# An attention-and-experts kernel: both column tiles of the weights-times-values products read all 128 key rows

## The chip, the cores and the metric

The kernel runs on one core of a Trainium2 chip. The metric is the device time of one execution in microseconds (us); lower is better.

## What is computed

Two parts follow one another. The first is a gated linear attention (an mLSTM): for 4 batches, 8 heads, 768 time steps and 40 features it runs the recurrence below. The second is a soft mixture of 8 experts with 4 slots each over the 3072 rows that the first part gives.

```python
for t in range(S):
    m_new = np.maximum(f_gate[:, :, t] + m, i_gate[:, :, t])
    f_stab, i_stab = np.exp(f_gate[:, :, t] + m - m_new), np.exp(i_gate[:, :, t] - m_new)
    C = f_stab * C + i_stab * outer(vt, kt)
    n = f_stab * n + i_stab * kt
    y[:, :, t] = sigmoid(o_gate[:, :, t]) * (C @ qt) / np.maximum(np.abs(n @ qt), 1.0)
...
logits = x @ phi
d = softmax(logits, over rows);  slot_input = d.T @ x
slot_out[e] = np.maximum(slot_input[e] @ w1[e], 0.0) @ w2[e]
out = softmax(logits, over slots) @ slot_out
```

## The kernel before

The recurrence is worked in chunks of 128 time steps. A step `i` of the main loop is one chunk of one batch: `c = i // 4` is the chunk, `i % 4` the batch, 24 steps in all (`NSTEP`). All 8 heads of a step go together as 4 pairs (`HP`), `j` is the pair and `e` the head in it. Within a chunk a query attends to the keys of its own chunk, up to its own time, by a matrix of weights; to everything earlier it attends through a state of 40 x 41 numbers a head (the last column carries the normaliser).

What one step does:

- `expo(i)` (L294): two products on TensorE (L302) build the logarithms of the decay weights in the PSUM tile `pe`, keys on the partitions, queries on the columns, in two halves of 64 queries. For the first 64 queries only keys 0 to 63 are worked out; rows 64 to 127 of that half of `pe` were set to -1e30 once, at the start (L173). ScalarE then takes the exponential of all 128 rows of both halves into `ew[i]` (L304), so that the rows of later keys hold zeros. From step 4 on, a further product (L312 and L313 in chunks 0 to 2, L316 after) and exponential (L317) give the decay of the state for each query. In chunks 0 to 2 the factors of these products, `LLt` and `RR`, are written by ScalarE (L267) and VectorE (L270) in the step before; later ones come by DMA.
- `scores(i)` (L331): keys times queries, 16 matmuls into `psc`. `mix(i)` (L345, VectorE) multiplies them into `ew[i]`.
- `mix_q(i)` (L340, GpSimd) multiplies the queries by the state's decay.
- `pv(i)` (L383): the products that the change touches. For each pair `j` it adds up, in a PSUM tile `ph` with the 128 queries on the partitions, the part from the state (L393, 104 rows, 82 columns, from step 4 on) and the part from the chunk's own keys (L398, one head at a time, 41 columns: 40 features of the values and the normaliser). The 128 queries are cut in two column tiles of 64 (`u`, `NT = 2`, `TW = 64`), which use the left and the right half of TensorE's columns (`tile_position=(0, 64 * u)`) and write the lower and the upper half of the partitions of `ph`. For `u = 0`, the first 64 queries, L398 reads only keys 0 to 63 (`k = LH = 64` rows); for `u = 1` it reads all 128.
- `post1`, `post2` (L403, L419, VectorE) and `gate` (L430, GpSimd) divide and gate the result; `xtr` (L438) transposes it (L444) and ScalarE copies it out (L447).
- `keys(i)` (L350, GpSimd) and `state(i)` (L362) give the state's increment: for each pair two products with 128 rows and 41 columns (L367 with 64 columns of weights into partitions 0 to 63 of `pst`, L369 with 40 into partitions 64 to 103). `state_ops` (L371) adds it to the state.
- Every fourth step the experts' part takes up four finished steps: `moe_logits` (L452), `moe_psl` (L505), transposes (L496, L522, L543).

The order of all instructions is written out by hand. The loop (L666) issues, in step `i`: loads, `expo(i+2)`, `mix(i+1)`, `gate(i-1)`, `mix_q(i+1)`, `keys(i+1)`, `state_ops(i-1)`, the experts' parts, `pv(i)`, `scores(i+2)`, `state(i)`, `xtr(i-1)`, then `post1(i)` and `post2(i)`. The last two steps stand after the loop (L745 on), with `pv` into the PSUM tiles `phe` and `bk`. After them come the experts' two layers (`up` L874, `down` L900) and the output (`combine` L922). Loads are issued on the SP queue.

Each float32 product appears in the trace as two passes, each with a weight load (LDWEIGHTS, engine PEld) and a MATMUL (engine PE). A pair `j` of `pv` from step 4 on thus has 4 passes of L393 and 8 of L398.

Of the kernel before, what the change touches and what calls it, by code (L numbers as in the profile page):

```python
# [16 lines left out]
LH = L // 2  # L17
NT = 2
TW = L // NT
# [3 lines left out]
V1 = D + 1  # L23
# [44 lines left out]
def kernel(ctx: ExitStack, tc: tile.TileContext, qk, kv, og, g0, g1, g2, consts, cb, w1, w2, out):  # L68
    nc = tc.nc
    P = 128  # L70
# [287 lines left out]
    def v_of(i, h):  # L358
        return KV[i % NK][:, DM + h * V1:DM + (h + 1) * V1]
# [23 lines left out]
    def pv(i, ph_=None):  # L383
        w = ew[i]
        if ph_ is None:
            ph_ = pp.tile([P, 512], F32, tag="ph", name=f"ph{i}")

        for j in range(HP):
            c0 = 2 * j * V1
            if i >= B:  # L390
                for u in range(NT):
                    z = slice(TW * u, TW * u + TW)
                    nc.tensor.matmul(ph_[z, c0:c0 + 2 * V1], w[0:104, 2, j, z], St[0:104, i % B, j], start=True, stop=False,  # L393
                                     tile_position=(0, TW * u))
            for e in range(2):
                for u in range(NT):
                    z, k = slice(TW * u, TW * u + TW), LH if TW * u < LH else P
                    nc.tensor.matmul(ph_[z, c0 + e * V1:c0 + (e + 1) * V1], w[0:k, e, j, z], v_of(i, 2 * j + e)[0:k],  # L398
                                     start=i < B, stop=i < B or e == 1, tile_position=(0, TW * u))
        phs[i] = ph_[:, 0:H * V1].rearrange("p (h d) -> p h d", h=H)  # L400
        nqs[i] = ph_[:, 512 - H:512]
# [208 lines left out]
    emit(nxt)  # L610
    state(0)
    pv(0, pp.tile([P, 512], F32, tag="pm", name="ph0", bufs=2))
    load_kv(3)
    emit(state_ops(0))
# [51 lines left out]
    for i in range(1, NL - 1):  # L666
# [40 lines left out]
        if i > GRP and i % GRP == 2:  # L707
            moe_acc(gi, psl)
        pv(i)
        scores(i + 2)  # L710
        state(i)
# [26 lines left out]
    i = NL - 1  # L738
# [13 lines left out]
    nc.gpsimd.memset(xy[:, DM:DM + 1], 1.0)  # L752
    nc.gpsimd.memset(xr[:, :, DM:DM + 1], 1.0)
    pv(i)
    scores(NL + 1)
    pl4 = moe_pl(gl - 1, "pm")
# [33 lines left out]
    j = NL + 1  # L790
# [279 lines left out]
```

## Time and profile before

| | |
|---|---|
| median of 3 runs | 370.34 us (365.2 to 373.87) |
| the profiled execution | 364.1 us |
| span of its instructions | 362.3 us |
| mean granted TensorE clock | 0.592 of 2.4 GHz |
| PE busy | 340.0 us (94%) |
| PEld busy | 239.8 us (66%) |
| VectorE, ScalarE, GpSimd busy | 108.7, 97.1, 77.2 us |

The span is what the profile shows; 1.8 us of the execution lie around it. PE is TensorE's matmuls and PEld its weight loads, which overlap them. Matmuls are pipelined, and the profile models their ends, so that a busy PE is not a PE at its peak: starts of successive matmuls say more than their durations. The granted clock has two levels here, 0.5 (1.2 GHz) and 1.0 (2.4 GHz).

### The profile page before, as it was taken

What the parts mean: (1) busy time and instruction counts of PE and PEld (TensorE: products, weight loads), DVE (VectorE), ACT (ScalarE), POOL (GpSimd) and SP (SyncE); (2) the same over time, 40 slices, a digit from 0 to 9 for tenths busy, and PEclk for the clock granted to TensorE, in tenths of its full rate; (3) what the DMA queues carried; (4) which work ended last, traced back from release to release, by engine and by line L of the source; (5) the groups of instructions that cost most, each with busy time, mean ns of one, the idle gap of its engine ahead of it and who ended that gap; (6) DMA issues with size and microseconds to landing.
All of it is one profiled execution on the core that took longest, in us unless ns stands there. A gap on an engine that the chain in (4) does not pass through costs nothing.

```text
span 362.3 us, 6383 instructions
## 1 busy us (share of the span) xinstructions
PE 340.0 (94%) x2609; PEld 239.8 (66%) x2609; DVE 108.7 (30%) x311; ACT 97.1 (27%) x234; POOL 77.2 (21%) x95
## 2 busy tenths in 40 slices
PE   5999988987989899999999999999999999999991
PEld 2777866756567677567677577677686677552681
DVE  7534304201423331213231214133141212233251
ACT  6734053031321303411221402232212200121041
POOL 4602334200213320203320204220233210011000
PEclk9556555555555558555555556578865555558996
DMA  8653435042134603414631613842504525390067
GB/s 246 195 167 111 145 125 175 30 133 71 60 85 139 203 18 121 136 47 144 192 100 50 207 29 108 276 134 80 190 17 145 183 62 193 118 352 3 2 214 224
DMA packets 27308, 47.36 MB, mean 131 GB/s; under 512 B 3168, under 2 KB 18400, under 8 KB 27280
## 3 DMA queue, kind: packets, MB, share of 16 engines
q1 hardware_dynamic: 27280, 46.96, 40.5%
q8 instruction: 21, 0.34, 0.4%
q14 instruction: 7, 0.06, 0.1%
HBM read 42.72 MB, written 4.23 MB: 130 GB/s over the span
## 4 chain that ended last, share of the span: by engine, by line
PE 75%; DVE 1%; ACT 1%; issue 1%; DVEq 0%
PE ph L398 25%; PE psc L338 9%; PE ph L393 7%; PE pe L302 4%; PE pt L444 4%; PE pst L367 3%; PE pso L905 3%; PE phh L877 2%; PE pl L452 2%; PE phe L398 2%; PE bk L398 2%; PE psl L505 2%; PE pq L316 1%; PE po L935 1%; PE bk L877 1%; PE pst L369 1%
## 5 line engine op out<-in xcount | busy, mean ns | idle before, releaser
L398 PE MATMUL ph<-KVt,ew 64*64 64x41 f32 x704 | 125.1, 302 | 0.0
L398 PEld LDWEIGHTS ph<-KVt,ew 64*64 64x64 f32 x704 | 94.4, 190 | 33.2 <-issue 11.8
L434 POOL TENSOR_TENSOR Xt<-sig,den 128x320 f32<-128x320 f32 x20 | 15.1, 756 | 176.2 <-DVE sig L423 98.4
L447 ACT COPY xT<-pt 128x384 f32<-128x384 f32 x23 | 11.0, 479 | 154.8 <-PE pt L444 154.8
L338 PE MATMUL psc<-KQt 64*128 64x128 f32 (+1 forms) x384 | 49.4, 434 | 0.4 <-DVE ew L348 0.4
L393 PE MATMUL ph<-St,ew 104*64 104x82 f32 x288 | 46.0, 342 | 1.0 <-DVE sig L423 1.0
L338 PEld LDWEIGHTS psc<-KQt 64*128 64x128 f32 (+1 forms) x384 | 42.3, 321 | 3.7 <-DVE ew L348 1.1
L393 PEld LDWEIGHTS ph<-St,ew 104*64 104x64 f32 x288 | 29.6, 197 | 10.4 <-issue 9.8
L348 DVE TENSOR_TENSOR ew<-psc,ew 128x1024 f32<-128x1024 f32 x24 | 29.3, 1223 | 21.4 <-PE psc L338 19.6
L407 DVE TENSOR_REDUCE ph<-ph 128x8 f32<-128x8 f32 x22 | 3.8, 172 | 98.2 <-PE ph L398 98.2
L304 ACT ACTIVATE ew<-pe 128x512 f32<-128x512 f32 x48 | 26.0, 593 | 23.5 <-PE pe L302 22.2
L343 POOL TENSOR_TENSOR ew<-KQt,ew 104x512 f32<-104x512 f32 x20 | 25.4, 1271 | 11.0 <-ACT ew L317 9.7
L302 PE MATMUL pe<-RRt,LLt 128*64 128x512 f32 (+1 forms) x24 | 12.9, 637 | 10.7 <-ACT LLt L267 7.9
L367 PEld LDWEIGHTS pst<-KVt,KRt 128*64 128x64 f32 x160 | 18.5, 221 | 4.5 <-issue 3.4
L367 PE MATMUL pst<-KVt,KRt 128*64 128x41 f32 x160 | 21.5, 310 | 0.0
L444 PE MATMUL pt<-cst,Xt 128*128 128x128 f32 x63 | 18.3, 433 | 0.0
L353 POOL TENSOR_TENSOR KRt<-KVt,rl 128x320 f32<-128x320 f32 x20 | 15.7, 787 | 9.6 <-ACT rl L325 9.4
L369 PE MATMUL pst<-KVt,KRt 128*40 128x41 f32 x160 | 16.1, 276 | 0.0
L302 PEld LDWEIGHTS pe<-RRt,LLt 128*64 128x64 f32 (+1 forms) x24 | 5.1, 234 | 15.1 <-ACT LLt L267 8.2
L378 DVE SCALAR_TENSOR_TENSOR St<-St,rl,pst 104x82 f32<-104x82 f32 x64 | 14.7, 292 | 0.0
L369 PEld LDWEIGHTS pst<-KVt,KRt 128*40 128x40 f32 x160 | 13.1, 170 | 0.0
L526 DVE TENSOR_REDUCE rmx<-pd 128x4 f32<-128x128 f32 x4 | 1.2, 292 | 39.6 <-PE pd L522 39.6
(230 smaller groups left out, 348.3 us busy)
## 6 DMA issues: line engine op xcount, KB each, us to landing
w<-in_w_dram SPq DMA_DIRECT2D x20, 512.0 KB, 5.0
KVt<-in_kv_dram SPq DMA_DIRECT2D x24, 324.0 KB, 3.1
KQt<-in_qk_dram SPq DMA_DIRECT2D x24, 320.0 KB, 3.8
w<-in_w_dram SPq DMA_DIRECT2D x10, 640.0 KB, 6.5
sig<-in_og_dram SPq DMA_DIRECT2D x6, 640.0 KB, 6.3
out_dram<-ob SPq DMA_DIRECT2D x5, 384.0 KB, 2.8
KQt<-in_w_dram SPq DMA_DIRECT2D x2, 640.0 KB, 6.0
out_dram<-ob SPq DMA_DIRECT2D x2, 512.0 KB
```

The costliest lines, as they stand in the source:

```text
L302: nc.tensor.matmul(pe[0:x, n], l[0:k, n * LH:n * LH + x], r[0:k, :, n * LH:n * LH + LH], start=True, stop=True)
L304: nc.scalar.activation(w[:, 0:2, :, n * LH:n * LH + LH].rearrange("p e j t -> p j e t"), pe[:, n].rearrange("p (j e) t -> p j e t", e=2), ...
L338: nc.tensor.matmul(psc[:, e, j], t[r0:r1, 1, j], t[r0:r1, 0, j], start=True, stop=True)
L343: nc.gpsimd.tensor_tensor(w, KQ[i % NQ][0:104, 0], w, ALU.mult)
L348: nc.vector.tensor_tensor(w, pscs.pop(i), w, ALU.mult)
L353: e.tensor_tensor(kr[i][:, 24:].rearrange("p (j e d) -> p j e d", e=2, d=D), KV[i % NK][:, 0:DM].rearrange("p (j e d) -> p j e d", e=2, d= ...
L367: nc.tensor.matmul(pst[0:64, j, 0:V1], kr[i][:, h * D:h * D + 64], v_of(i, h), start=True, stop=True)
L369: nc.tensor.matmul(pst[64:64 + D, j, V1:], kr[i][:, 24 + h * D:24 + (h + 1) * D], v_of(i, h), start=True, stop=True)
L393: nc.tensor.matmul(ph_[z, c0:c0 + 2 * V1], w[0:104, 2, j, z], St[0:104, i % B, j], start=True, stop=False, tile_position=(0, TW * u))
L398: nc.tensor.matmul(ph_[z, c0 + e * V1:c0 + (e + 1) * V1], w[0:k, e, j, z], v_of(i, 2 * j + e)[0:k], start=i < B, stop=i < B or e == 1, til ...
L434: e.tensor_tensor(x_of(i)[:, h0 * D:h1 * D].rearrange("p (h d) -> p h d", d=D), s1_of(i)[:, h0:h1], dens[i][:, h0:h1].unsqueeze(2).broadca ...
L444: nc.tensor.transpose(pt[:, kc, :], x[:, o:o + P], ident)
```

## The change

For the first column tile, L398 takes all 128 rows of weights and values in place of the first 64. The rows that are added multiply the values of keys 64 to 127 by the zeros that stand in `ew` for them. Nothing else is changed: the same number of instructions, in the same order, on the same tiles.

```diff
             for e in range(2):
                 for u in range(NT):
-                    z, k = slice(TW * u, TW * u + TW), LH if TW * u < LH else P
-                    nc.tensor.matmul(ph_[z, c0 + e * V1:c0 + (e + 1) * V1], w[0:k, e, j, z], v_of(i, 2 * j + e)[0:k],
+                    z = slice(TW * u, TW * u + TW)
+                    nc.tensor.matmul(ph_[z, c0 + e * V1:c0 + (e + 1) * V1], w[:, e, j, z], v_of(i, 2 * j + e),
                                      start=i < B, stop=i < B or e == 1, tile_position=(0, TW * u))
```

## Rows read from the trace of the kernel before

**Rows 1.** The page: engines' busy time, clock in 40 slices, DMA total.

```profile
PE 340.0 (94%) x2609; PEld 239.8 (66%) x2609; DVE 108.7 (30%) x311; ACT 97.1 (27%) x234; POOL 77.2 (21%) x95
...
PEclk9556555555555558555555556578865555558996
...
DMA packets 27308, 47.36 MB, mean 131 GB/s; under 512 B 3168, under 2 KB 18400, under 8 KB 27280
```

**Rows 2.** The page: the chain that ended last, share of span by line.

```profile
PE ph L398 25%; PE psc L338 9%; PE ph L393 7%; PE pe L302 4%; PE pt L444 4%; PE pst L367 3%; PE pso L905 3%; PE phh L877 2%; PE pl L452 2%; PE phe L398 2%; PE bk L398 2%; PE psl L505 2%; PE pq L316 1%; PE po L935 1%; PE bk L877 1%; PE pst L369 1%
```

**Rows 3.** PE groups by shape: count | busy us, mean ns of one | idle before.

```profile
L398 PE MATMUL ph<-KVt,ew 128*64 128x41 f32 x352 | 72.6, 304 | 0.0
L398 PE MATMUL ph<-KVt,ew 64*64 64x41 f32 x352 | 71.8, 300 | 0.0
```

**Rows 4.** Timeline of PE, one `pv` (step 11): start us, duration us, line.

```profile
163.16 0.54 PE L393 MATMUL ph<-St,ew 104*64 104x82 f32 x4
163.63 1.43 PE L398 MATMUL ph<-KVt,ew 64*64 64x41 f32 x7
164.73 0.40 PE L393 MATMUL ph<-St,ew 104*64 104x82 f32 x1
164.85 0.31 PE L398 MATMUL ph<-KVt,ew 128*64 128x41 f32 x1
164.92 0.56 PE L393 MATMUL ph<-St,ew 104*64 104x82 f32 x3
165.41 0.43 PE L398 MATMUL ph<-KVt,ew 64*64 64x41 f32 x2
...
170.44 0.58 PE L338 MATMUL psc<-KQt 64*128 64x128 f32 x2
```

**Rows 5.** Timeline of PE, `pv` of step 2, without a state part.

```profile
34.95 5.93 PE L398 MATMUL ph<-KVt,ew 64*64 64x41 f32 x32
```

**Rows 6.** Timeline of PE, `state` of one step.

```profile
159.66 0.31 PE L367 MATMUL pst<-KVt,KRt 128*64 128x41 f32 x1
159.72 0.27 PE L369 MATMUL pst<-KVt,KRt 128*40 128x41 f32 x1
...
159.98 0.52 PE L367 MATMUL pst<-KVt,KRt 128*64 128x41 f32 x3
160.43 0.47 PE L444 MATMUL pt<-cst,Xt 128*128 128x128 f32 x1
```

**Rows 7.** Timeline of PEld, a weight load of the same `state`.

```profile
159.70 0.23 PEld L367 LDWEIGHTS pst<-KVt,KRt 128*64 128x64 f32 x1
```

**Rows 8.** L398 in stretches of the loop: us, PE busy (count), PEclk, DMA.

```profile
25.60:29.00 3.40, 3.31 (x28) 1.00 0.72 282
...
134.80:141.60 6.80, 3.04 (x24) 1.00 0.57 177
...
240.60:247.40 6.80, 4.08 (x32) 1.00 0.57 177
247.40:250.90 3.50, 0.00 (x0) 0.51 0.00 0
```

**Rows 9.** Timeline of PE around `pv` of step 17, clock raised.

```profile
242.65 0.36 PE L393 MATMUL ph<-St,ew 104*64 104x82 f32 x4
...
247.23 0.62 PE L338 MATMUL psc<-KQt 64*128 64x128 f32 x4
```

**Rows 10.** Timeline of PE, start of `pv` of step 19, clock raised.

```profile
262.65 0.36 PE L393 MATMUL ph<-St,ew 104*64 104x82 f32 x4 [0.58 <-DVE sig L423]
```

**Rows 11.** The loop in stretches: us, then busy us of PE, PEld, DVE, ACT, POOL.

```profile
15.00:61.40 46.40, 44.55 (x283) 32.96 (x280) 17.23 (x30) 16.20 (x38) 14.73 (x15) 0.54 0.39 125
61.40:150.10 88.70, 82.24 (x594) 58.91 (x593) 22.91 (x68) 23.68 (x64) 15.91 (x17) 0.54 0.33 104
150.10:296.90 146.80, 145.83 (x1112) 105.78 (x1108) 37.23 (x121) 32.60 (x79) 34.88 (x42) 0.57 0.38 121
296.90:312.50 15.60, 15.60 (x105) 11.83 (x101) 4.34 (x13) 1.35 (x5) 0.00 (x0) 0.50 0.43 147
```

**Rows 12.** Timeline of PE, first matmuls of step 5.

```profile
73.51 1.12 PE L302 MATMUL pe<-RRt,LLt 128*64 128x512 f32 x2 [0.92 <-ACT LLt L267]
```

## The prediction

> **What bounds the kernel.** I read the page first. TensorE is busy for 94% of the span and no other engine for more than 30% [rows 1]; the chain that ended last is made of TensorE's lines, L398 first with 25% of the span and 2% more in each of the last two steps, L393 with 7% [rows 2]. So what TensorE saves in `pv` is saved at the end, until something else is late.
>
> Next, where `pv` loses time. The groups by shape don't show it: a pass of L398 with 64 rows has a mean of 300 ns, one with 128 rows 304 ns [rows 3]. These are latencies of a pipeline; the starts count, and the timeline has them [rows 4]. A pair begins its L398 at 163.63, the next at 165.41: 1.78 us for 12 passes. In it the last L398 of a pair (128 rows, second column tile, 164.85) does not hold up the next pair's L393 (104 rows, first column tile), of which one started at 164.73 and three more from 164.92 on: there two column tiles run side by side. Ahead of the 64-row pass at 165.41, on the other hand, the engine lets the L393 passes run out. Without the state part, 32 passes take 5.93 us, 0.19 us each [rows 5].
>
> `state` shows the other way to run: 128 rows throughout, two column tiles, 41 columns as in L398. Of its L367, three passes begin at 159.98, the last at 159.98 + 0.52 - 0.31 = 160.19, so 0.105 us apart, while L369 goes through the other column tile among them (159.66, 159.72). From the last start it takes 0.24 us until work of another shape begins (L444 at 160.43) [rows 6]. My reading: passes on 64 and on 128 rows exclude one another, and each change between them costs a drain; the same rows on two column tiles do not.
>
> **The change, part by part.**
>
> *Rows added.* 384 passes get 128 rows: 4 ns each by the means [rows 3], 1.5 us if nothing hid it; at the rate of `state` it is in the 0.105. The zeros are written already; no instruction, wait or transfer is added or moved. For the sum: 0.
>
> *Drains removed.* Each column tile has, for a pair, 4 passes of L398 at 0.105 = 0.42 us, and 2 of L393. A steady rate of L393 (82 columns, 104 rows) is nowhere to be seen. Bounds: at least the 0.105 of 41 columns, at most the 0.19 us between its starts at 164.73 and 164.92 [rows 4]. Taken: 0.14, between the two, since the first row of a burst carries a start. 0.42 + 0.28 = 0.70 us a pair (0.63 to 0.80) for 1.78.
>
> Sum for all of `pv` at 1.2 GHz: before, 20 steps of 7.28 us (163.16 to 170.44 [rows 4]) and 4 of 5.93 [rows 5] = 169 us. Of the 768 passes of L398 (24 steps of 32) some 143 fall into six stretches with a raised clock (28, 24 and 32 in the three shown [rows 8]), 19%; there `pv` takes 4.58 us (242.65 to 247.23 [rows 9]), 37% less. So 169 x (1 - 0.19 x 0.37) = 157 us in this execution. After, at 1.2 GHz: 80 pairs x 0.70 + 16 pairs x 0.42 + 24 ends x 0.24 = 56 + 7 + 6 = 69 us (63 to 77). Gain 88 us (80 to 94): 364.1 - 88 = 276 us.
>
> *What is late next.* Steps shrink from some 12 or 13 us to 9. In steps 10 to 21 VectorE, ScalarE and GpSimd are busy 37, 33 and 35 us [rows 11], some 3 us in each of the 12 steps; none becomes the bound. Two short waits surface. Where TensorE was fast, `pv` waited 0.58 us for `post2` (L423) of the step before [rows 10]; five steps can have that: 3 us. And the gates' scans, which VectorE does in the first steps, come nearer: 3 us taken, 0 to 10 as bounds (the larger is the 1.85 + 6.46 us in which PE is idle from 15.0 to 150.1 [rows 11], once more). The 0.92 us in which L302 waits for ScalarE's L267 [rows 12] stay. Transfers: 47.36 MB [rows 1] in 240 us are 197 GB/s; the shares of 0.33 to 0.43 now [rows 11] grow by half; hidden. Together 276 + 6 = 282 us with the clock no better than before.
>
> *The clock.* The granted clock is at 0.5 nearly everywhere in the loop [rows 1]. Each of the six raised stretches holds much of a `pv` and the clock falls by its end (24 and 32 passes of L398 in those from 134.80 and 240.60); the next rise comes after a stretch without L398 (none from 247.40 to 250.90), in which scores, `state` and transposes stand [rows 8]. So the drained `pv` is what loses the clock. With the change `pv` runs as `state` does, and a raised clock should hold through it. Price: the 37% of `pv` above. At 1.2 GHz the loop then has 69 us of `pv`, and of other work: 297.5 us from 15.0 to 312.5 less 9 idle [rows 11] less 157 of `pv` = 131 us, of which some 13 had the raised clock already (the six stretches are 31 us, 18 of them `pv`): 118. 37% of 187 us is 69 us if all is raised. I take 14 of the 24 steps, for from step 10 on nothing waits for L267, and before that each step keeps its idle 0.92 us: 14/24 x 69 = 40 us. 282 - 40 = 242 us.
>
> **A rule against it.** From 159.70 to 159.93 L367 loads weights on all 128 rows while L369's matmul of 159.72, also on 128 rows, is in flight [rows 6, 7]. The Trainium skill, "TensorE: Matmul & The Clock Gate", Part 3 (The mechanism), says that a weight load overlaps with matmuls in flight only if its row group is another one. By that rule the two column tiles, now on the same rows, would take turns, and the time would be that of the third rival; the trace does not agree with it here.
>
> **Rivals.**
> - *The clock stays as it was.* For it: the slices from 61 to 131 us show 5 throughout [rows 1], and a step keeps four or five changes of shape at 0.24 us. Against: rises follow dense work. 282 us, or 276 if no wait surfaces.
> - *Raised through the whole loop:* 282 - 69 = 213 us. Against all of it: the waits of [rows 10, 12] weigh more then.
> - *The column tiles take turns:* every pass waits for the one before, 0.13 us as for two passes on the same 64 rows (165.41: 0.43 - 0.30). 12 x 0.13 = 1.56 for 1.78 on 80 pairs, 8 x 0.13 = 1.04 for 5.93/4 = 1.48 on 16: 25 us, 339 us. Against it: [rows 4, 6].
> - *The change doesn't do what it says:* the pauses come not from the row count but, say, from adding to columns of `ph` that are still being written, which `state` does only within two passes. Then 1.5 us are added: 366 us. Against it: L393's passes also add to the same columns and start 0.19 us apart.
> - *Slower:* the pauses stay and the raised stretches go. Their 31 us become 31/0.63 = 49 at 1.2 GHz: 364 + 18 = 382 us. It decides only if the gain of 88 us fails; nothing shown speaks for it.
> - *A chain of waits takes over,* first the prefetch of keys and values, whose buffers come free only after `state`: if it holds the 20 later steps at 10 us in place of 9, 282 + 20 = 302 us. Against it: the low shares of DMA.
>
> **How the numbers follow.** Chances: clock raised in a good part of the loop (220 to 265 us) 0.58; clock as before (270 to 285) 0.20; raised nearly throughout (210 to 220) 0.08; waits (290 to 315) 0.05; turns 0.04; no effect 0.03; slower 0.02. The time predicted is that of the first, 242 us. It stands against the profiled execution's 364.1, which lies 1.7% under the median of 370.34. The range is 214 to 284: it takes in the clock as before and half of the case with everything raised, and leaves out 0.18. All but the last two cases are faster by over 2% (about what a measurement of this kernel can tell from no change): 0.95; within 2% 0.03; slower 0.02.
>
> **What would show it.** Right: in a `pv` at 1.2 GHz, L398 starts every 0.105 us on each column tile, with the next pair's L393 among them, and `pv` takes about 3.0 us from its first matmul to the scores (1.9 without a state part). The row of granted clocks shows 8s and 9s in the loop's later slices. Mean durations of L398 hardly change. A new row among the waits: L393 for L423. Wrong: a pair that still takes over 1.5 us, or pauses between heads (the row count is not the cause); a `pv` of 3.0 us with 5s throughout (282 us); idle time of PE in every step with DMA or GpSimd as its releaser (302 us).

## The result

| | before | after |
|---|---|---|
| median of 3 runs | 370.34 us | 199.34 us |
| the profiled execution | 364.1 us | 199.34 us |
| span | 362.3 us | 197.6 us |
| mean granted TensorE clock | 0.592 | 0.903 |

The ratio of after to before, without the longest execution of either (223.2 us at a mean granted clock of 0.782, where the other two have 0.903 and 0.921, and 373.87 us), is 0.541 (95% interval 0.524 to 0.558): 46% less time. That is faster, as forecast, but below the range of 214 to 284 us.

The page of after, for [rows 1] (engines' busy time, granted clock in 40 slices):

```profile
PE 172.0 (87%) x2609; PEld 124.9 (63%) x2609; DVE 109.8 (56%) x311; ACT 95.9 (49%) x234; POOL 76.7 (39%) x95
...
PEclk9958999655555999999999999999999999999995
```

The other engines are busy for as long as before, to 1.2 us, and the count of instructions is the same. What went is TensorE's time, and the row of clocks shows 9 where before it had 5.

The chain that ended last, for [rows 2], and the group of L398, for [rows 3]:

```profile
PE psc L338 9%; PE ph L398 7%; PE ph L393 7%; PE pe L302 5%; PE pso L905 5%; PE pt L444 4%; PE pst L367 4%; DMA w<-in_w_dram 3%; PE po L935 3%; PE pl L452 2%; PE bk L877 2%; PE phh L877 2%; PE psl L505 2%; PE pq L316 2%; PE pq L312 1%
```

```profile
L398 PE MATMUL ph<-KVt,ew 128*64 128x41 f32 x704 | 34.7, 234 | 0.3 <-PE pq L313 0.3
```

L398 fell from 25% of a long chain to 7% of a short one. Its mean went only from some 300 to 234 ns, and that is the clock (where the clock is low, from 37 to 63 us, the median is 308 ns); its busy time went from 125.1 us (page of before) to 34.7. The gain lies in the starts.

The timeline of PE in `pv` of step 5, at 1.2 GHz, for [rows 4] (start us, duration us):

```profile
48.51 0.54 PE L393 MATMUL ph<-St,ew 104*64 104x82 f32 x4
48.84 0.60 PE L398 MATMUL ph<-KVt,ew 128*64 128x41 f32 x8
49.23 0.52 PE L393 MATMUL ph<-St,ew 104*64 104x82 f32 x4
49.54 0.60 PE L398 MATMUL ph<-KVt,ew 128*64 128x41 f32 x8
...
51.47 2.08 PE L338 MATMUL psc<-KQt 64*128 64x128 f32 x16
```

The same of step 14, at 2.4 GHz, for [rows 9]:

```profile
109.78 0.36 PE L393 MATMUL ph<-St,ew 104*64 104x82 f32 x4
109.98 0.38 PE L398 MATMUL ph<-KVt,ew 128*64 128x41 f32 x8
110.18 0.34 PE L393 MATMUL ph<-St,ew 104*64 104x82 f32 x4
...
111.42 1.16 PE L338 MATMUL psc<-KQt 64*128 64x128 f32 x16
```

A pair takes 0.70 us at 1.2 GHz (48.84 to 49.54) for 1.78, and the whole `pv` 2.96 us for 7.28; raised it is 1.64 us for 4.58. The scores behind it (L338, 16 matmuls) show what the clock alone does: 2.08 and 1.16 us.

After in stretches, for [rows 11] (us, then busy us of PE, PEld, DVE, ACT, POOL, then clock, DMA share, GB/s):

```profile
14.20:36.40 22.20, 18.38 (x282) 14.12 (x281) 16.37 (x28) 15.36 (x38) 14.37 (x16) 0.96 0.82 255
36.40:63.70 27.30, 23.53 (x241) 17.36 (x242) 9.87 (x24) 10.63 (x27) 5.30 (x6) 0.50 0.43 142
63.70:154.20 90.50, 85.25 (x1567) 66.16 (x1563) 56.12 (x179) 47.09 (x120) 46.10 (x55) 1.00 0.91 273
154.20:197.60 43.40, 34.28 (x483) 21.51 (x481) 17.81 (x60) 11.99 (x31) 2.46 (x4) 0.95 0.67 217
```

Steps 0 to 3, but for the first 2 us, and everything from the end of step 6 on run raised; the clock is low from 36.4 to 63.7 us. Ahead of that TensorE stands still twice within 3 us, and in it again, before the first matmul of a step, as in [rows 12]. Timeline of PE:

```profile
33.39 0.22 PE L367 MATMUL pst<-KVt,KRt 128*64 128x41 f32 x1 [0.76 <-ACT St L376]
...
35.42 0.79 PE L302 MATMUL pe<-RRt,LLt 128*64 128x512 f32 x2 [0.92 <-ACT LLt L267]
...
44.88 1.12 PE L302 MATMUL pe<-RRt,LLt 128*64 128x512 f32 x2 [0.92 <-ACT LLt L267]
...
58.45 1.09 PE L302 MATMUL pe<-RRt,LLt 128*64 128x512 f32 x2 [2.85 <-DVE ph L407]
...
67.91 0.79 PE L302 MATMUL pe<-RRt,LLt 128*64 128x512 f32 x2 [1.24 <-ACT LLt L267]
```

The last of these waits lies behind the rise, and the clock stays up through it and through two more, of 0.92 and 0.63 us, in the next two steps.

### The profile page after: what moved, and what is told of

Read it like the earlier page. It is cut to its first block, busy times and chain, and to the rows that moved or that the text cites. A ratio compares the mean times of both kernels' runs of the same rounds, so it can differ in the third digit from the quotient of the medians.

```text
span 197.6 us, 6383 instructions
## 1 busy us (share of the span) xinstructions
PE 172.0 (87%) x2609; PEld 124.9 (63%) x2609; DVE 109.8 (56%) x311; ACT 95.9 (49%) x234; POOL 76.7 (39%) x95
## 4 chain that ended last, share of the span: by engine, by line
PE 62%; DVE 4%; DMA 3%; ACT 2%; issue 1%; SPq 1%; DVEq 0%; ACTq 0%
PE psc L338 9%; PE ph L398 7%; PE ph L393 7%; PE pe L302 5%; PE pso L905 5%; PE pt L444 4%; PE pst L367 4%; DMA w<-in_w_dram 3%; PE po L935 3%; PE pl L452 2%; PE bk L877 2%; PE phh L877 2%; PE psl L505 2%; PE pq L316 2%; PE pq L312 1%
## 5 line engine op out<-in xcount | busy, mean ns | idle before, releaser
L398 PE MATMUL ph<-KVt,ew 128*64 128x41 f32 x704 | 34.7, 234 | 0.3 <-PE pq L313 0.3
L398 PEld LDWEIGHTS ph<-KVt,ew 128*64 128x64 f32 x704 | 31.6, 151 | 1.3 <-PE pq L313 0.7
L338 PE MATMUL psc<-KQt 64*128 64x128 f32 (+1 forms) x384 | 31.3, 309 | 0.5 <-DVE ew L348 0.5
L393 PE MATMUL ph<-St,ew 104*64 104x82 f32 x288 | 27.2, 268 | 1.9 <-DVE sig L423 1.9
L338 PEld LDWEIGHTS psc<-KQt 64*128 64x128 f32 (+1 forms) x384 | 26.3, 208 | 2.9 <-DVE ew L348 1.2
L393 PEld LDWEIGHTS ph<-St,ew 104*64 104x64 f32 x288 | 16.3, 150 | 8.5 <-issue 7.8
L302 PE MATMUL pe<-RRt,LLt 128*64 128x512 f32 (+1 forms) x24 | 10.3, 512 | 11.3 <-ACT LLt L267 8.5
L367 PE MATMUL pst<-KVt,KRt 128*64 128x41 f32 x160 | 14.4, 244 | 0.8 <-ACT St L376 0.8
L367 PEld LDWEIGHTS pst<-KVt,KRt 128*64 128x64 f32 x160 | 12.0, 150 | 3.5 <-POOL gf L221 0.9
L302 PEld LDWEIGHTS pe<-RRt,LLt 128*64 128x64 f32 (+1 forms) x24 | 4.1, 180 | 15.7 <-ACT LLt L267 9.6
L317 ACT ACTIVATE ew<-pq 104x512 f32<-104x512 f32 x20 | 12.0, 601 | 0.0
L369 PE MATMUL pst<-KVt,KRt 128*40 128x41 f32 x160 | 11.3, 220 | 0.0
L407 DVE TENSOR_REDUCE ph<-ph 128x8 f32<-128x8 f32 x22 | 3.7, 168 | 11.3 <-PE ph L398 11.3
L423 DVE SCALAR_TENSOR_TENSOR sig<-sig,ph 128x320 f32<-128x320 f32 x22 | 9.8, 449 | 0.0
```

What stands on the lines that cost most here:

```text
L302: nc.tensor.matmul(pe[0:x, n], l[0:k, n * LH:n * LH + x], r[0:k, :, n * LH:n * LH + LH], start=True, stop=True)
L338: nc.tensor.matmul(psc[:, e, j], t[r0:r1, 1, j], t[r0:r1, 0, j], start=True, stop=True)
L367: nc.tensor.matmul(pst[0:64, j, 0:V1], kr[i][:, h * D:h * D + 64], v_of(i, h), start=True, stop=True)
L398: nc.tensor.matmul(ph_[z, c0 + e * V1:c0 + (e + 1) * V1], w[:, e, j, z], v_of(i, 2 * j + e), start=i < B, stop=i < B or e == 1, tile_posit ...
```

## The experiments

Three questions were open: what in the 64 rows cost the time, what keeps the clock up, and what bounds the kernel now. Each run stands beside runs of the kernel before on the same chip. The first four kernels were run once each.

**Is it the number of rows, or a class of rows?** The first column tile gets 65 rows.

```diff
-                    z = slice(TW * u, TW * u + TW)
+                    z, k = slice(TW * u, TW * u + TW), LH + 1 if u == 0 else P
```

(In this and the next kernels the matmul reads rows `0:k` again.)

> L398 reads 65 rows for the first column tile and 128 for the second. Theory (a drain stands between passes of two row classes, up to 64 rows and above; the number itself does not matter): as with 128 rows, pv 3.0 us at 1.2 GHz and 1.6 raised, 195 to 225 us. Rival (any difference in the number of rows costs the drain): as before the change, pv 7.3 us at 1.2 GHz, about 365 us.

Measured: 213.18 us, before 368.06. Timeline of PE, one `pv` at 1.2 GHz:

```profile
60.57 0.60 PE L398 MATMUL ph<-KVt,ew 65*64 65x41 f32 x8
60.96 0.53 PE L393 MATMUL ph<-St,ew 104*64 104x82 f32 x4
61.27 0.61 PE L398 MATMUL ph<-KVt,ew 65*64 65x41 f32 x8
```

0.70 us a pair again (60.57 to 61.27), with 65, 104 and 128 rows side by side. One row more than 64 gives the whole gain in `pv`, and the time lies among those of the changed kernel; the equal count of 128 is not what matters.

**Can passes of 64 rows run side by side?** Both column tiles get 64 rows in L398.

```diff
-                    z = slice(TW * u, TW * u + TW)
+                    z, k = slice(TW * u, TW * u + TW), LH
```

> L398 reads 64 rows for both column tiles, which leaves the products of the later 64 queries with keys 64 to 127 out of the result. Theory (changes of row class cost): in steps 0 to 3, which have no state part, no change is left in pv and it takes 1.9 us at 1.2 GHz or 1.1 raised, as with 128 rows; in later steps two changes per pair are left, between L393 with 104 rows and L398: 0.70 + 2 x 0.27 = 1.24 us a pair, pv 5.1 us at 1.2 GHz, and 260 to 330 us in all. Rival (passes of 64 rows cannot run side by side on two column tiles): pv of steps 0 to 3 stays at 5.9 us (4.1 raised) and the time near 365 us.

Measured: 289.00 us. Timeline of PE, `pv` of step 1, which has no state part, then of step 5; then the row of clocks:

```profile
22.20 1.94 PE L398 MATMUL ph<-KVt,ew 64*64 64x41 f32 x32
24.06 0.58 PE L338 MATMUL psc<-KQt 64*128 64x128 f32 x2
...
58.76 0.54 PE L393 MATMUL ph<-St,ew 104*64 104x82 f32 x4
59.23 0.66 PE L398 MATMUL ph<-KVt,ew 64*64 64x41 f32 x8
59.82 0.54 PE L393 MATMUL ph<-St,ew 104*64 104x82 f32 x4
...
62.98 0.58 PE L338 MATMUL psc<-KQt 64*128 64x128 f32 x2
```

```profile
PEclk9555565555555555885555575558855555589995
```

Where all passes have 64 rows, 32 of them take 1.86 us (22.20 to 24.06), 0.058 us each; in the changed kernel the 12 passes of a pair, with 104 and 128 rows, take 0.70 us, 0.058 each too. So 64 rows are not slow. Where L393 with 104 rows stands between them, a pair takes 1.06 us (58.76 to 59.82): 0.36 more than 0.70 for two changes, 0.18 each. That was expected at 0.27; the theory holds and the price was too high.

**Drains apart from overlap.** Two kernels do the first column tile for all pairs and then the second, so that nothing runs side by side; one has the rows of before (shown), the other 128 (`k` is `P`).

```diff
-        for j in range(HP):
-            c0 = 2 * j * V1
-            if i >= B:
-                for u in range(NT):
-                    z = slice(TW * u, TW * u + TW)
+        for u in range(NT):
+            z, k = slice(TW * u, TW * u + TW), LH if u == 0 else P
+            for j in range(HP):
+                c0 = 2 * j * V1
+                if i >= B:
...
-            for e in range(2):
-                for u in range(NT):
-                    z = slice(TW * u, TW * u + TW)
+                for e in range(2):
```

> The rows of before (64 for the first column tile), but in pv the first column tile is done for all four pairs, then the second: no side by side, and 8 changes of row class a pv in place of 16. Theory: 8 x 0.70 us for the passes one after the other + 8 changes at 0.2 to 0.27 us: pv 7.3 to 8.0 us at 1.2 GHz, 365 to 390 us. Rival (the pauses come from alternating the column tiles or from adding to columns still being written, not from rows): the same time as the next kernel.

> The same order as the kernel before this one, with 128 rows in both column tiles: no change of row class and nothing side by side. Theory: pv 8 x 0.70 + 0.24 = 5.8 us at 1.2 GHz, half of that and a little more raised, so that the side by side is worth 2.9 us of the 4.3 and the drains the rest: 235 to 290 us by the clock. Rival (128 rows alone, with no overlap, give all of it): pv 3.0 us at 1.2 GHz, 200 us.

Measured: 332.95 and 233.28 us. Timeline of PE of the first, `pv` of step 5 at 1.2 GHz, first column tile, then second:

```profile
66.29 0.54 PE L393 MATMUL ph<-St,ew 104*64 104x82 f32 x2
66.75 0.65 PE L396 MATMUL ph<-KVt,ew 64*64 64x41 f32 x4
67.33 0.53 PE L393 MATMUL ph<-St,ew 104*64 104x82 f32 x2
...
71.17 0.51 PE L393 MATMUL ph<-St,ew 104*64 104x82 f32 x2
71.48 0.59 PE L396 MATMUL ph<-KVt,ew 128*64 128x41 f32 x4
71.87 0.51 PE L393 MATMUL ph<-St,ew 104*64 104x82 f32 x2
...
73.40 1.01 PE L338 MATMUL psc<-KQt 64*128 64x128 f32 x6
```

Of the second, `pv` of one step at 1.2 GHz, and the row of clocks:

```profile
60.38 0.53 PE L393 MATMUL ph<-St,ew 104*64 104x82 f32 x2
...
65.77 1.01 PE L338 MATMUL psc<-KQt 64*128 64x128 f32 x6
```

```profile
PEclk9755999998557555899999999999999999999996
```

In one kernel and one `pv`, the six passes of a pair in one column tile take 1.04 us with 64 rows (66.29 to 67.33; L396 is the L398 of the other kernels) and 0.70 with 128 (71.17 to 71.87): 0.34 for two changes, 0.17 each. With 128 rows and hardly any overlap (a few passes, where one column tile follows the other) `pv` takes 5.39 us (60.38 to 65.77), for 5.8 expected. Against 2.96, the side by side is worth 2.4 us, and of the 4.3 us that the change saves in a `pv` at 1.2 GHz the rest is 1.9. Both rivals fall. The times lie below what was expected, that of the second by 2 us, that of the first by 32: its `pv` takes 7.11 us (66.29 to 73.40), just under the 7.3, and its mean granted clock was 0.639, for 0.582 in the kernel before on that chip. The pair of before can now, after the fact, be put together: 0.70 of streaming, four changes at 0.17, and the L398 passes of one column tile (4 x 0.105) no longer beside the other's: 0.70 + 0.68 + 0.42 = 1.80, for 1.78 measured [rows 4]. By this sum the overlap that the kernel before had lost is 4 x 0.42 = 1.7 us in a `pv`, less than the 2.4 above, since its L393 did run side by side.

The rows of clocks say more. With 64 rows everywhere a `pv` at 1.2 GHz is shorter than in this last kernel (58.76 to the scores at 62.98 is 4.22 us, for 5.39), and yet that kernel runs at 5 in most of its loop and this one at 9 in most of it: 289 against 233 us. So the low clock goes with the changes of row class, which only the first has in `pv`, and not with the length of `pv`. Nor does it go with the number of rows at work: 65 rows in the first column tile ran at a mean clock of 0.833, the kernel before, with 64, at 0.582 on the same chip.

**One head with 64 rows.**

```diff
+                    z, k = slice(TW * u, TW * u + TW), LH if u == 0 and j == 2 and e == 0 else P
```

> 128 rows everywhere but in the first column tile of one head of eight, which keeps 64: two changes of row class a pv in place of 16. Theory (each change costs a pause of its own, 0.15 to 0.3 us, and two of them do not lose the clock): pv longer by 0.3 to 0.5 us, 24 times: 204 to 226 us. Rival (one change is enough to lose the clock): over 250 us.

Measured: 233.56 us (226.90 and 240.21), above the 204 to 226 expected; 211.46 for the changed kernel on the same chip. Timeline of PE, `pv` of step 11, raised:

```profile
113.47 0.36 PE L393 MATMUL ph<-St,ew 104*64 104x82 f32 x4 [0.63 <-DVE sig L423]
...
115.49 0.38 PE L338 MATMUL psc<-KQt 64*128 64x128 f32 x2
```

A raised `pv` takes 2.02 us for 1.64 (113.47 to 115.49): 0.38 for two changes and the overlap lost by one head, within what was expected. 24 of them are 9 us of the 22; the rest goes with the clock. It was low from 37.5 to 105.7 us of the span here, and in the changed kernel on this chip from 36.6 to 97.9 with a rise of 6.8 us in between. Two changes a step do not keep it down for good; that they delay it rests on one profile of each.

**Does the drained `pv` lose the clock?** Old rows again from step 12 on.

```diff
+                    z, k = slice(TW * u, TW * u + TW), LH if u == 0 and i >= 12 else P
```

> 128 rows as in the changed kernel up to step 11, 64 rows for the first column tile again from step 12 on. Theory (the pauses in pv lose the raised clock): raised before step 12 and at 0.5 for most of the rest; steps 12 to 21 go back to some 12 us from 5.4, 260 to 285 us. Rival (the clock, once up, is held by the other work): 12 x (4.58 - 1.64) = 35 us more, 230 to 245 us, PEclk 9 to the end.

Measured: 297.01 us (294.13 and 299.89), above the 285 expected: the clock had been low from 38.2 to 99.6 us, with a rise of 6.8 us in between, before any old row ran. L398 in stretches from step 10 on (us, PE busy and count, clock):

```profile
99.60:116.70 17.10, 7.14 (x96) 1.00 0.85 262
116.70:120.10 3.40, 0.00 (x0) 0.50 0.41 124
120.10:126.90 6.80, 4.08 (x32) 1.00 0.49 163
126.90:130.30 3.40, 0.00 (x0) 0.51 0.12 28
130.30:144.00 13.70, 7.31 (x58) 1.00 0.65 218
```

The first old `pv` runs raised from 111.4 us; the clock falls right behind it, comes and goes twice, and from 144.0 us stays at 0.5 to the end of the last step (243 us). The changed kernel on this chip has the same low stretch in steps 4 to 9 (its row of clocks stands below), and from 97.9 us on its clock stays up to the end of its work, at 203.8 us. So the old rows are what differs, and the rival, 230 to 245 us, falls.

**What bounds the first ten steps.** In the changed kernel the factors of a later step (L267, L270) are issued ahead of the transposes' copies and the gates' scans.

```diff
         state(i)
+        ops = chunk_list(i + 3)
         if i > GRP - 1 and i % GRP == 1:
             moe_dT(gi)
...
-        for ops, plan in later:
-            emit(ops, plan[i] if i < len(plan) else 0)
+        emit(ops)
+        for gops, plan in later:
+            emit(gops, plan[i] if i < len(plan) else 0)
...
-        ops = chunk_list(i + 3)
```

> The changed kernel again, on the same chip as the next ones. 195 to 215 us; pv 2.96 us where the clock is at 1.2 GHz and 1.64 where it is raised.

> The changed kernel, with ScalarE's and VectorE's factors of a later step (L267, L270) issued ahead of the transposes' copies and of the gates' scans rather than behind them. If the waits of L302 for L267 (8.5 us) and for L407 (2.85 us) bound the first ten steps: 8 to 11 us less than the changed kernel on the same chip, more if the clock no longer falls there (up to 20 us). Rival (those copies then come late instead, or the transfers bound these steps): no difference.

Measured: the changed kernel 211.46 us (207.58 to 218.32), the other 183.66 (182.20 to 189.22). The rows of clocks, the changed kernel on this chip, then the other:

```profile
PEclk9859999556955555556999999999999999999995
```

```profile
PEclk9955899999999999999999999999999999999985
```

28 us less by the medians, 25 by the lowest times, more than the 20 expected at most. The waits of PE account for 6 us of it (13.1 us of idle above 0.1 us, for 18.8); the rest goes with the clock, which after its rise at 19.9 us does not fall until the end of the work, though single waits are left, the longest of 0.91 us.

The same edit on the kernel before:

> The kernel before (64 rows for the first column tile), with the factors L267 and L270 issued early as in e6. If the pauses in pv alone keep the clock down there: only the waits go (the 7.9 us of L302 for L267 and 2.85 for L407), 352 to 362 us, PEclk 5 in the first ten steps as before. Rival (the idle of L302 is what lost the clock in either kernel): the clock rises in steps 4 to 9, 320 us or less.

Measured: 350.62 us (345.61 to 366.68), just under the 352 expected, before 372.51. The row of clocks:

```profile
PEclk9555565555565585555588955555555555558997
```

Much of the idle goes (14.6 to 6.1 us), the clock stays at 5 but for short rises: with a drained `pv` in every step, idle between the steps decides little. With a packed one it decided much. The gain, 22 us by the medians and 15 by the lowest times (360.91 and 345.61), is above the 8.5 of idle; what makes up the rest is open.

**Idle or a late operand?** Nothing is moved, the wait stays, but TensorE works on zeros in it.

```diff
         hs = r.rearrange("p (j e) t -> p e j t", e=2)
+        if 4 < i < CD * B:
+            for _ in range(3):
+                nc.tensor.matmul(pe[:, 1].rearrange("p h t -> p (h t)"), wz[:, 0:P], wz, start=True, stop=True)
```

> The changed kernel, with three matmuls of 512 columns on zeros issued ahead of L302 in steps 3 to 9, in the time in which it waits for L267; nothing else is moved, and the wait stays. Theory (idle of TensorE between the steps, not a late operand, loses the clock): the clock stays raised from the first rise on, 188 to 200 us against 199 to 218 of the changed kernel, in spite of 21 matmuls more. Rival (the clock falls for another reason there): 207 to 225 us.

Measured: 196.60 us (191.26 to 197.50), as expected. Timeline of PE, and the row of clocks:

```profile
41.82 0.59 PE L303 MATMUL pe<-wz 128*128 128x512 bf16 x2
42.69 0.78 PE L305 MATMUL pe<-RRt,LLt 128*64 128x512 f32 x2 [0.28 <-ACT LLt L267]
```

```profile
PEclk9856999999856999999999999999999969999996
```

The clock stays raised through steps 3 to 5 and falls for 10 us behind the 2.2 us that are left of the wait for L407 (it ends at 51.68 us, in step 6). All four runs lie below each run of the changed kernel (207.58 us at least on one other chip, 198.66 on another): 3 to 15 us less by the medians, by 21 matmuls that compute nothing. Across chips the size is loose; that the clock stays up where the idle was filled is in the row of the one profile.

**What bounds the later steps.** On top of the early factors, `post` goes ahead of L526 and L527 in every fourth step; then also the load of queries and keys goes ahead of that of keys and values.

```diff
         if i > GRP and i % GRP == 2:
+            emit(p1)
+            p1 = []
             ops += moe_e0_ops(gi, "pm")
```

> As e6, and in every fourth step VectorE does post1 and post2 ahead of the two operations on the transposed logits (L526, L527) rather than among them. If L393's waits for L423 (0.63 us three times, 0.91, 0.26 and 0.18 in e6) bound those steps: 2 to 4 us less than e6, 179 to 182 us. Rival (the transfers, whose share is 0.93 in steps 10 to 21, take it back): as e6.

```diff
+        load_qk(i + 3)
         if i > 1:
             load_kv(i + 2)
-        load_qk(i + 3)
```

> As e7, and the load of queries and keys of step i+3, whose buffer is free, is issued ahead of the load of keys and values of step i+2, which waits on the queue for the state products of the step before. If the waits of L338 for these loads (0.88 and 0.25 us in e6) come from that queue: 1 to 2 us less than e7, 177 to 181 us. Rival (the transfers are full): no difference.

Measured: 183.66 us (182.99 to 191.73) and 180.59 (180.29 to 180.72), before 372.51. Timeline of PE of the first, two scores, then the loop of the second as a stretch (busy us of PE, PEld, DVE, ACT, POOL, clock, DMA share):

```profile
73.29 1.16 PE L338 MATMUL psc<-KQt 64*128 64x128 f32 x16 [1.12 <-DVE sig L423]
...
126.07 1.16 PE L338 MATMUL psc<-KQt 64*128 64x128 f32 x16 [0.80 <-DMA KQt<-in_qk_dram]
```

```profile
14.00:133.00 119.00, 115.61 (x2048) 90.10 (x2046) 82.12 (x227) 73.54 (x187) 66.95 (x75) 0.98 0.95 285
```

The early `post` alone brings nothing, as its rival had it: the waits of L393 for L423 go from steps 11, 15 and 19, and scores wait for late operands instead. With the load first, those waits go too, and the version is the fastest of all: 180.59 us, which is 0.485 of the kernel before on the same chip by the medians (372.51) and 0.50 of that kernel's lowest time there (360.91), and its four runs lie within 0.5 us. Its loop keeps PE busy for 97% and the DMA engines for 95%; no wait of TensorE for a transfer is left in it, but there is little room on either.

## Why the prediction was wrong

**Right: what `pv` does.** "0.70 us a pair" was 0.70, the `pv` of "about 3.0 us" at 1.2 GHz was 2.96, and the rates taken from `state` held [rows 6]. The reading behind it, that passes of 64 and of more rows exclude one another, was put to the test and holds: 65 rows are as good as 128, 64 rows alone are as fast, and a change costs 0.17 to 0.18 us. The Trainium skill, "TensorEngine Tiling (Array Packing)", Key Properties, says that a change of tiling mode drains the engine while a change of tile does not; these runs agree, and put the price at 0.17 us at 1.2 GHz. The Trainium skill, "TensorE: Matmul & The Clock Gate", Part 3 (The mechanism), lets a weight load overlap with matmuls in flight only on another row group. That does not hold here as the prediction takes it: on the same rows, a pair takes 0.70 us on two column tiles side by side, as long as it takes on one of them alone (71.17 to 71.87). Of the rivals, turns, no effect and slower are out.

**Wrong: the clock.** The step that failed is the one from 282 to 242 us. Its mechanism was right, drained work loses the raised clock and packed work holds it; the old rows from step 12 on and the order with 128 rows and no overlap show it. But its terms were mis-sized: it gave the clock 40 us, and the numbers below come to 78.

- "I take 14 of the 24 steps": the clock was low for 27.3 us only, steps 4, 5 and most of 6, so some 21 of 24 ran raised. The reason given, that up to step 9 every step keeps its idle 0.92 us, was half right: with that idle taken out or filled the clock does not fall there (the early and the filled version show it), but in steps 7 to 9 it stayed up through waits of 1.24, 0.92 and 0.63 us. On the other chip, with nearly the same waits, it was low in most of steps 4 to 9, 54.5 us, and that execution took 211.27 us. What decides between the two courses is open, and with it some of the size of the miss: of seven executions of the changed kernel two, 218.32 and 223.20 us, lie inside the range.
- "37% of 187 us": 37% is the price of the drained `pv` [rows 4, 9], and drains shrink less than streaming (from the last start of L398 to the scores 0.24 us at 1.2 GHz and 0.16 raised, worked out as in the prediction). Packed work gives back more: `pv` 2.96 to 1.64 is 45%, the scores 2.08 to 1.16 are 44%. With 21 of 24 steps and 44%, 187 us of work give back 72 us, not 40: 282 - 72 = 210.
- The end was not counted. From the end of the last `pv` on the kernel took 49.8 us before and 43.4 after. Before, the first part of it ran at 0.5 (stretch of the kernel before):

```profile
312.50:329.40 16.90, 16.11 (x106) 7.70 (x109) 7.22 (x31) 4.50 (x13) 1.73 (x3) 0.50 0.74 254
```

After, the clock is up when it begins. 210 - 6 = 204 us. Of the 5 us that still lie above 199.3 the waits, taken at 6, cover 2: they came to 4 (idle of PE above 0.1 us: 14.6 before, 18.7 after). The other 3 are open. A slip in the sum matters little: the 18 raised us put down as `pv` are L398 alone; the 143 passes at 4.58 us for 32 are 20 us, which moves the result by under 1 us.

So the chances were wrong more than the mechanism: "raised nearly throughout" had 0.08, and its time, 213, still carried the 37%. The case was there; it was held to be a corner because the waits of [rows 12] were thought to spoil it in every step.

**The waits.** L393 for L423 came as foreseen, 0.63 us in three steps, 1.9 us for the 3 taken. L302's waits in the first steps, for which 3 us more were taken, went from 10.7 to 11.3 us. "None becomes the bound" held for the engines. For the transfers "hidden" was true, with little to spare: a share of 0.91 from 63.7 to 154.2 us, for 0.38 before, and no wait of TensorE for them there.

## What to carry to other kernels

Count changes of TensorE's row class (64 rows on the one side, 65 to 128 on the other, as far as these runs go) in the order of the matmuls: the rows that the shorter contraction saved were worth nothing in time here, while each change cost a drain and the side by side of column tiles. Zeros that fill up to the class of the neighbours cost nothing where they stand ready, as here. When a change packs TensorE's work, work out the time at both clocks, with each kind of work's own price at each, and not a mean: the packed work may hold the raised clock, and then the work behind it gets faster too (44 to 45% less time here). After that, look in the row of clocks for idle times at which it falls: here those of the first steps cost 28 us by the medians, of which 6 were idle, though other waits as long went by with the clock up.

## What the runs showed of the hardware

- A change between 64 rows and more costs 0.17 to 0.18 us at 1.2 GHz; a pass with 65 rows runs beside those with 104 and 128.
- On two column tiles, 32 passes with 64 rows take 1.86 us at 1.2 GHz, 12 passes with 104 and 128 rows 0.70 us: 0.058 us a pass in both.
- A low granted clock went with changes of row class, not with the length of `pv`: a `pv` of 5.39 us without changes ran in a kernel with a mean clock of 0.887, one of 4.22 us with eight changes in one with 0.609.
- With the waits of the first steps (0.92 us in several, 2.85 us in one) taken out, the changed kernel was 28 us faster by the medians, of which 6 were idle and the rest went with the clock; 21 matmuls on zeros in that idle time won back 3 to 15, by the chip that it is compared with. Single waits of up to 1.24 us also went by with the clock up.
